# Loading the q and k weights once and copying them by TensorE, and chaining later loads to compute stages, in a fused attention and gMLP block

## The chip, the cores and the metric

The kernel runs on one core of a Trainium2 chip. The core has TensorE (PE, matmuls into the eight banks of PSUM), VectorE (DVE), ScalarE (ACT), GpSimd (POOL) and SyncE (SP). Each runs its own list of instructions in order and waits on semaphores for the others; 16 DMA engines move data between device memory (HBM) and the on-chip memory (SBUF), on transfers that SP and ACT issue here. The metric is the device time of one execution in microseconds (us), and the median of several runs is compared.

## The reference

A block on x of shape (1, 2048, 448), in bf16: sliding, dilated attention with 16 heads of 28 columns, and a gMLP mixer, each behind a layer norm and with a residual.

```python
h = x + A(layernorm(x), wqkv, wo)
h2 = h + B(layernorm(h), w_in, w_sp, b_sp, w_out)

# A: per head, token i attends to i, i-2, ..., i-14 (W=8, dil=2)
idx = pos[:, None] - (jnp.arange(W) * dil)[None, :]
logits = einsum('bhsd,bhswd->bhsw', q, k[..., idx, :]) * 28 ** -0.5
o = einsum('bhsw,bhswd->bhsd', softmax(where(idx >= 0, logits, -1e9)), v[..., idx, :])
return o.reshape(B, S, D) @ wo

# B: F = 1792, Fh = 896
z = gelu(x @ w_in)
z1, z2 = z[..., :Fh], layernorm(z[..., Fh:])
g = einsum('ts,bsf->btf', w_sp, z2) + b_sp[None, :, None]
return (z1 * g) @ w_out
```

## The kernel before

**Tiling.** The 2048 tokens are two halves of 1024. Block u holds 128 tokens of the first half and block u+8 those of the second; the two are worked on together. After the layer norm, TensorE transposes the pair (L643) so that `xh` holds the 448 features as seven chunks of 64, the first half's in partitions 0 to 63 and the second half's in 64 to 127. A matmul over 64 features runs for s = 0 on the lower partitions and for s = 1 on the upper ones. So every weight that multiplies `xh` must stand in both partition halves: q, k (`wqp`, `wkp`), v (`wv`) and `w_in`. A halo of the last 16 tokens of the first half (`xhalo`, `thalo`) goes ahead of the second half's tokens.

**Stages.** (1) Loads, the layer norm of each pair (`bn1`, `rs1` on POOL at L611/L612, `nrm1`), transposes and their eviction. (2) q and k in three token chunks (`mmk`, `mmq`, L738), v for each of nine attention tiles (`mmv`, L778). Per tile: logits (`mml`, L813), exp on ACT (`exp`, L826), a band mask on DVE (`mask`, L833), row sums (`mmr`, L842), ln and exp for the reciprocal, the weighted sum (`mmo`, L862) and its scaling (`ot`, L880). (3) Output projection (`mmy`, L918), residual (`h`), second layer norm and transposes. (4) z2 (`mmz2`, L938, gelu `ge`) and z1 (`mmz1`, L982, `gz1`), the third layer norm; then the big product with `w_sp` (L1019), the gating on DVE (`ua`, `um`) and the output matmuls (`wo`, L1048), stored block by block.

**What sets the order.** A planner in the kernel's own Python lists tasks with durations, dependencies and priorities, and lays them on the five engines; the order so found is the order of the instructions. `OFF`, `TU`, `WPEN`, `MPEN`, `SEED` and `SIGMA` set the priorities. Several evictions may go to either of two or three engines (`alts`). The planner's own estimates are not waits: an instruction waits only for semaphores that its reads and writes need (`Sched.issue`).

**Weights of q and k.** `ld_w("qk", s)` loads the same 448 x 896 columns twice, once into each partition half of `stqk` (which lies in the later `z2p`), one on SP's queue and one on ACT's. Eight copies (`rp`, L702 to L706, on ACT, DVE or POOL) then spread each head's 28 columns to a pitch of 32 in `wqp` and `wkp`.

**Later loads.** `w_in` comes in four transfers of 784 KB (two column halves, two partition halves), `w_sp` in 32 transposing transfers into `wspT_lo` and `wspT_hi`. At the end a list `pace` adds planner dependencies, so that these loads take their place in SP's list behind certain stages:

```python
pace = [by[n % i] for i in range(NT) for n in (("exp%d_0", "ot%d") if i else ("ot%d",))]
later = [t_win[1, 0], t_win[1, 1], t_win[0, 0], t_win[0, 1]] + [t_wsp[b][0] for b in S_ORDER]
for t, d in zip(later, pace):
    t.deps.append(d)
```

No semaphore stands behind these dependencies: on the chip SP issues the transfers as soon as it reaches them.

## Time and profile before

| | |
|---|---|
| median of 3 runs | 274.48 us (272.98 to 274.57) |
| the profiled execution | 273.63 us |
| its span, first to last instruction | 271.7 us |
| mean granted TensorE clock | 0.962 |
| bytes read from HBM / written | 9.20 MB / 1.84 MB |

The span is what the profile shows; the 1.9 us between it and the execution's time lie around it. In the profile's rows a line such as L738 is a line of the kernel above; "out<-in" are names of tiles (`reg` is the shared memory in which `wqp`, `kT`, `E` and others lie; `z2p` holds the staged weights at the start). "[1.60 <-issue]" means that the engine stood idle 1.60 us before the row and that the profile shows nothing it waited for. The granted clock is a share of TensorE's full speed.

These pieces of the chain of waits (start, us, engine and line) date the later stages: z2, the first products with `wspT_lo`, and the long run of them.

```profile
102.76 1.46 PE psum L938 x14
...
120.62 2.75 PE psum L938 x28
123.37 10.59 PE psum L982 x98
...
134.51 0.38 PE psum L1019
...
151.86 10.74 PE psum L1019 x49
...
178.57 1.32 PE psum L1048 x7
```

### The profile page before, as it was taken

How to read it: one execution, taken by the hardware profiler on the slowest of the kernel's cores; microseconds unless marked ns; L12 is line 12 of the kernel's file. 1: busy time of each engine (PE TensorE's matmuls, PEld its weight loads, DVE VectorE, ACT ScalarE, POOL GpSimd, SP SyncE). 2: the span in 40 equal slices, each digit the busy share in tenths (PEclk: the TensorE clock that was granted, in tenths of full speed). 3: DMA queues.
4: the chain of work that ended last, by engine and by line, in shares of the span. 5: the costliest groups of instructions: out<-in, count | busy, mean ns of one | idle time of the engine just before them, and what ended most of it. 6: DMA issues, size and time to landing. Idle time of an engine off the chain costs nothing.

```text
span 271.7 us, 6639 instructions
## 1 busy us (share of the span) xinstructions
PE 253.5 (93%) x2987; PEld 129.5 (48%) x2999; DVE 149.5 (55%) x283; ACT 90.7 (33%) x100; POOL 33.2 (12%) x78
## 2 busy tenths in 40 slices
PE   7279897799999989999999999999999999999995
PEld 2076465344556655544454444444444444444442
DVE  2396993356897877999963133324334423343333
ACT  0068835655489758657657300000000000000000
POOL 7253410000112111232311000000000000000000
PEclk9759997799999979999999999999999999999999
DMA  6960299999900000006444335321000100001002
GB/s 183 250 196 17 54 212 203 165 172 147 188 20 2 2 5 2 0 17 205 72 92 86 80 77 80 77 56 51 2 0 0 51 19 0 0 17 53 0 0 69
DMA packets 43733, 19.85 MB, mean 73 GB/s; under 512 B 34537, under 2 KB 43577, under 8 KB 43705
## 3 DMA queue, kind: packets, MB, share of 16 engines
q1 hardware_dynamic: 42632, 18.11, 33.1%
q10 hardware_dynamic: 1072, 1.32, 1.9%
q8 instruction: 23, 0.38, 0.6%
q14 instruction: 6, 0.04, 0.1%
HBM read 9.20 MB, written 1.84 MB: 41 GB/s over the span
## 4 chain that ended last, share of the span: by engine, by line
PE 85%; DVE 5%; DMA 4%; issue 2%; ACT 2%; POOL 1%; SPq 0%
PE psum L1019 35%; PE psum L738 11%; PE psum L938 8%; PE psum L1048 8%; PE psum L982 8%; PE psum L918 4%; DMA xhalo<-in_A_x_dram 4%; PE psum L813 3%; PE psum L778 3%; PE psum L643 2%; PE psum L862 2%; DVE st L621 1%; ACT reg L826 1%; DVE tring L632 1%; PE psum L842 1%
## 5 line engine op out<-in xcount | busy, mean ns | idle before, releaser
L1029 DVE TENSOR_TENSOR ub<-psum,reg 128x512 bf16<-128x512 f32 x28 | 19.4, 692 | 73.4 <-PE psum L1019 73.4
L1019 PE MATMUL psum<-reg,z2p 128*128 128x512 bf16 x218 | 48.7, 379 | 0.3
L1019 PE MATMUL psum<-wspT_lo,z2p 128*128 128x512 bf16 x218 | 48.4, 379 | 0.4 <-issue 0.2
L1019 PEld LDWEIGHTS psum<-reg,z2p 128*128 128x128 bf16 x224 | 21.9, 98 | 26.2
L1019 PEld LDWEIGHTS psum<-wspT_lo,z2p 128*128 128x128 bf16 x224 | 21.7, 98 | 26.1 <-issue 0.4
L738 PE MATMUL psum<-xh,reg 64*128 64x128 bf16 (+3 forms) x336 | 29.8, 338 | 1.1 <-DVE xh L683 0.9
L1048 PE MATMUL psum<-reg 128*128 128x448 bf16 x112 | 22.3, 352 | 0.0
L938 PE MATMUL psum<-w_in,xh 64*128 64x448 bf16 x224 | 22.3, 349 | 0.0
L606 ACT ACTIVATE reg<-psum 128x896 bf16<-128x896 f32 (+4 forms) x20 | 16.8, 842 | 14.7 <-PE psum L738 8.6
L982 PE MATMUL psum<-xh,w_in 64*128 64x512 bf16 x196 | 21.5, 375 | 0.0
L738 PEld LDWEIGHTS psum<-xh,reg 64*128 64x128 bf16 x336 | 15.8, 110 | 10.6 <-issue 1.1
L621 DVE BATCH_NORM_STATS2 st<-x_tm 128x6 f32<-128x448 bf16 x32 | 19.5, 608 | 2.0 <-DMA x_tm<-in_A_x_dram 1.9
L826 ACT ACTIVATE reg<-psum 128x928 bf16<-128x928 f32 x18 | 17.1, 947 | 8.5 <-PE psum L778 5.9
L954 DVE BATCH_NORM_STATS2 st<-z2p 128x6 f32<-128x448 bf16 x32 | 17.6, 604 | 2.6 <-ACT z2p L948 2.6
L611 POOL TENSOR_SCALAR rs<-mv 128x2 f32<-128x2 f32 x24 | 6.1, 252 | 103.4 <-DVE mv L622 78.2
L948 ACT ACTIVATE z2p<-psum 128x896 bf16<-128x896 f32 x16 | 14.7, 917 | 9.6 <-PE psum L938 9.2
L612 POOL TENSOR_TENSOR rs<-rs,nhalf 128x2 f32<-128x2 f32 x24 | 17.6, 732 | 2.0
L632 DVE TENSOR_SCALAR tring<-x_tm,mv,rs 128x448 bf16<-128x448 bf16 x32 | 15.0, 490 | 3.4 <-POOL rs L612 3.2
L992 ACT ACTIVATE reg<-psum 128x1024 bf16<-128x1024 f32 x14 | 14.3, 1023 | 7.1 <-PE psum L982 7.1
L1048 PEld LDWEIGHTS psum<-reg 128*128 128x128 bf16 x112 | 11.0, 98 | 10.6
L938 PEld LDWEIGHTS psum<-w_in,xh 64*128 64x128 bf16 x224 | 10.9, 94 | 10.1 <-issue 0.8
L778 PE MATMUL psum<-reg,xh 64*64 64x448 bf16 x252 | 14.9, 378 | 0.5 <-DVE xh L608 0.5
(62 smaller groups left out, 229.3 us busy)
## 6 DMA issues: line engine op xcount, KB each, us to landing
w_in<-in_B_w_in_dram SPq DMA_DIRECT2D x4, 784.0 KB, 12.4
out_dram<-tring SPq DMA_DIRECT2D x16, 112.0 KB, 1.7
x_tm<-in_A_x_dram SPq DMA_DIRECT2D x15, 112.0 KB, 8.7
z2p<-in_A_wqkv_dram SPq DMA_DIRECT2D x1, 784.0 KB, 10.2
z2p<-in_A_wqkv_dram ACTq DMA_DIRECT2D x1, 784.0 KB, 11.6
reg<-in_B_w_out_dram SPq DMA_DIRECT2D x1, 784.0 KB, 4.8
reg<-in_B_b_sp_dram SPq DMA_DIRECT2D x1, 512.0 KB, 3.6
reg<-in_A_wqkv_dram ACTq DMA_DIRECT2D x1, 392.0 KB, 7.3
```

The lines of the kernel that those rows point to most:

```text
L612: iss("pool", lambda e: e.tensor_tensor(dst, dst, nh, ALU.pow), reads=rr + [r_nhalf], writes=rr)
L621: iss("dve", lambda e: e.bn_stats(st[:, b, :], x_tm[:, b, :]), reads=[r_x[b]], writes=[rl[b]])
L632: iss("dve", lambda e: e.tensor_scalar(tring[:, h[0], :].rearrange("p (c s f) -> p s c f", c=NC7, s=2)[:, n], x_tm[:, b, :].rearrange("p ( ...
L738: iss("pe", lambda e, c=c, s=s, gi=gi, lhs=lhs: e.matmul(psum[:, bk[s] * 512 + cw * gi:bk[s] * 512 + cw * gi + cw], lhs, xh[64 * s:64 * s ...
L778: iss("pe", lambda e, c=c, s=s, w=w: e.matmul(psum[64 * w:64 * w + 64, bk[s] * 512:bk[s] * 512 + D], xh[64 * s:64 * s + 64, c, a + w:a + w ...
L826: iss("act", lambda e: e.activation(E[:, es[0], 2 * n:2 * n + 2, :], pair_view(lb, 0, 8 * JW), AF.Exp, scale=SCALE), reads=[r_bank[lb[0]], ...
L938: iss("pe", lambda e, c=c, s=s: e.matmul(psum[:, zb[s] * 512:zb[s] * 512 + D], xh[64 * s:64 * s + 64, c, HALO + 128 * u:HALO + 128 * u + 128],
L954: iss("dve", lambda e, b=b: e.bn_stats(st3[:, b, k, :], z2p[:, b, D * k:D * k + D]), reads=[r_z2[b][k]], writes=[r_st3[b][k]])
L982: iss("pe", lambda e, c=c, s=s: e.matmul(psum[:, bk[s] * 512:bk[s] * 512 + 512], w_in[64 * s:64 * s + 64, c, 128 * f:128 * f + 128], xh[64 ...
L1019: iss("pe", lambda e, b=b: e.matmul(psum[:, gb[0] * 512:gb[0] * 512 + 512], z2p[:, b, 128 * f:128 * f + 128], src[:, b, 512 * (tc % 2):512 ...
L1029: iss("dve", lambda e: e.tensor_tensor(ub[:, us_[0], :], psum[:, gb[0] * 512:gb[0] * 512 + 512], bb[:, 512 * tc:512 * tc + 512], ALU.add), ...
L1048: iss("pe", lambda e, f=f: e.matmul(psum[:, wb[0] * 512:wb[0] * 512 + D], z1p[f][:, 128 * m:128 * m + 128], w_out[:, f, :], start=(f == 0) ...
```

## The change

Four things change.

1. The q and k weights are loaded once, 128 features to a partition row: 384 features in one transfer on ACT's queue (`wqk0`), the last 64 on SP's (`wqk1`). The halo moves to second place on SP.
2. A 128 x 128 matrix `dup` with ones on the diagonal and 64 off it is made on POOL. A matmul with half of it as the stationary operand puts 64 features into both partition halves of PSUM: 14 matmuls of 448 columns (`dpk`, `dpq`). Eight evictions (`rp`, now on ACT or DVE) write them to `wkp` and `wqp`. The q/k matmuls now wait for all four pieces of a weight.
3. `w_in` comes in eight transfers (four or three chunks of 64 features). Each load of two chains, `w_in` then the first half of `w_sp`, and bias, `w_out` then the second half of `w_sp`, now waits on semaphores: for the landing of the load before it in its chain and for one stage of compute. The first chain's stages are `exp`, `mask`, `ot` of the tiles in turn, the second's `ge`, `gz1` and `ua`.
4. The planner's priorities have other values, so the order of work changes on all engines.

```diff
-WPEN = 189.727
+WPEN = 200
...
-SEED, SIGMA = 806416, 0.5
+SEED, SIGMA = 242706, 1.0
...
-TU = 7.616
+TU = 7.37
...
+    def mark(self, eng):
+
+        m = Res("mark")
+        m.writes = {eng: self.cnt.get(eng, 0)}
+        return m
...
                     t.emit()
+                    if t.mark is not None and not t.nbytes:
+                        t.mark.append(self.marker(t.eng))
...
-        stqk = z2flat[:, 0:NC7 * 2 * D].rearrange("p (c n) -> p c n", c=NC7)
+        stqk = z2flat[:, 0:4 * 2 * D].rearrange("p (c n) -> p c n", c=4)
...
             def em():
-                key, _ = iss(eng, fn, reads=reads, writes=writes, prod="dma", inc=16)
+                rd = list(reads)
+                for w in t.waits:
+                    if w.nbytes:
+                        rd.append(w.mark)
+                    else:
+                        rd += w.mark
+                key, n = iss(eng, fn, reads=rd, writes=writes, prod="dma", inc=16)
+                t.mark = Res("mark")
+                t.mark.writes = {key: n}
...
+        def ld_win(z, prio):
+            for s in range(2):
+                for c0, c1 in ((0, 4), (4, 7)):
+                    t = dma("sp", "win%d_%d%d" % (z, s, c0), lambda e, s=s, c0=c0, c1=c1: e.dma_start(
+                        w_in[64 * s:64 * s + 64, c0:c1, FH * z:FH * z + FH],
...
-        ld_w("qk", 0, "sp", 0.02)
-        ld_w("qk", 1, "act", -10.0)
-        t_xhalo = dma("sp", "xhalo", lambda e: e.dma_start(xhalo[:, :], X[ST - 16:ST, :]), 16 * D * 2, prio=0.03, writes=[r_xhalo])
+        t_xhalo = dma("sp", "xhalo", lambda e: e.dma_start(xhalo[:, :], X[ST - 16:ST, :]), 16 * D * 2, prio=0.01, writes=[r_xhalo])
+        t_w["qk", 0] = dma("act", "wqk0", lambda e: e.dma_start(
+            stqk[:, 0:3, :], A_wqkv[0:384, 0:2 * D].rearrange("(c p) n -> p c n", p=128)),
+            384 * 2 * D * 2, prio=-11.0, writes=[r_wqk[0]], bw=300.0)
+        t_w["qk", 1] = dma("sp", "wqk1", lambda e: e.dma_start(stqk[0:64, 3, :], A_wqkv[384:448, 0:2 * D]),
+                           64 * 2 * D * 2, prio=0.02, writes=[r_wqk[1]])
...
+        c_dup = cst("c_dup", [(lambda e: e.memset(dup[:], 0.0), [], [r_dup])] + [
+            (lambda e, d=d: e.affine_select(dup[:], dup[:], [[1, 128]], ALU.not_equal, 1.0, base=d, channel_multiplier=-1),
+             [r_dup], [r_dup]) for d in (0, 64, -64)], 1.2, prio=-98.8)
...
-            for g in range(4):
-                tk = []
-
-                def em(p=p, g=g, tk=tk):
-                    c0 = 112 * g + (D if p == "k" else 0)
-                    copy(tk[0].eng, (wqp if p == "q" else wkp)[:, :, 128 * g:128 * g + 128]
+            for j in range(4):
+                bk, tk = [], []
+                hs = range(2 if j < 3 else 1)
+                c0 = D if p == "k" else 0
+
+                def em(j=j, bk=bk, hs=hs, c0=c0):
+                    for h in hs:
+                        iss("pe", lambda e, h=h: e.matmul(psum[:, bk[h] * 512:bk[h] * 512 + D], dup[64 * h:64 * h + 64, :],
+                                                          stqk[64 * h:64 * h + 64, j, c0:c0 + D]),
+                            reads=[r_wqk[j // 3], r_dup], writes=[r_bank[bk[h]]])
+                tm = add("dp%s%d" % (p, j), "pe", 0.2, em, deps=[t_w["qk", j // 3], c_dup], prio=4.0 + n + 0.1 * j,
+                         acq=[("ps", 2, bk)], mode="P", nmm=2)
...
-                             t_wp[p][g0:g0 + ng],
+                             t_wp[p],
...
-        pace = [by[n % i] for i in range(NT) for n in (("exp%d_0", "ot%d") if i else ("ot%d",))]
-        pace += [by["ge%d_%d" % (u, k)] for u in range(3) for k in range(2)]
-        later = [t_win[1, 0], t_win[1, 1], t_win[0, 0], t_win[0, 1]] + [t_wsp[b][0] for b in S_ORDER]
-        for t, d in zip(later, pace):
-            t.deps.append(d)
+
+        def chain(loads, steps):
+            assert len(steps) >= len(loads)
+            for n, t in enumerate(loads):
+                t.deps.append(steps[n])
+                t.deps += loads[n - 1:n] if n else []
+                t.waits += [steps[n]] + (loads[n - 1:n] if n else [])
+                steps[n].mark = steps[n].mark or []
+        pace = [by[n % i] for i in range(NT) for n in ("exp%d_0", "mask%d", "ot%d")]
+        later = t_win[1] + t_win[0] + [t_wsp[b][0] for b in S_ORDER]
+        chain(later, pace)
```

On PE the start of the program reads so before (L643 and L676 are the transposes of the first tokens and of the halo, L738 q/k, L778 v, L813 logits):

```order
L600 MATMUL psum<-warm 128x512 x16
L643 MATMUL psum<-ident,tring 128x128 x7
L676 MATMUL psum<-ident,thalo 128x16 x7
L738 MATMUL psum<-xh,reg 128x128 x112
L778 MATMUL psum<-reg,xh 64x448 x28
L813 MATMUL psum<-reg 64x58 x48
L643 MATMUL psum<-ident,tring 128x128 x7
L813 MATMUL psum<-reg 64x58 x16
```

and so after the change, where L739 is the copying with `dup`, L782 q/k, L822 v and L857 logits:

```order
L632 MATMUL psum<-warm 128x512 x16
L675 MATMUL psum<-ident,tring 128x128 x7
L708 MATMUL psum<-ident,thalo 128x16 x7
L739 MATMUL psum<-z2p,dup 128x448 x12
L822 MATMUL psum<-reg,xh 64x448 x28
L739 MATMUL psum<-z2p,dup 128x448 x2
L782 MATMUL psum<-xh,reg 128x128 x56
L675 MATMUL psum<-ident,tring 128x128 x7
L782 MATMUL psum<-xh,reg 128x128 x56
L822 MATMUL psum<-reg,xh 64x448 x28
L857 MATMUL psum<-reg 64x58 x32
```

The v matmuls of the first tile moved ahead of q/k, inside the copying; the second transposes moved between k and q, and the second v matmuls ahead of the logits.

On SP, from the last `wo` load on, with the semaphores each waits for, before (L887 `wo`, L544 `w_in`, L899 `w_sp`):

```order
L887 DMA reg<-in_A_wo_dram 28x4x448 [waits sem_q23]
L544 DMA w_in<-in_B_w_in_dram 64x7x896 x4
L899 DMA_TRANSPOSE wspT_lo<-in_B_w_sp_dram 128x1024 x16
L1000 DMA reg<-in_B_b_sp_dram 128x2048 [waits sem_pe,sem_q24]
L998 DMA reg<-in_B_w_out_dram 128x7x448 [waits sem_q45]
```

and after, where `sem_q` with a number is the landing of an earlier load and `sem_act`, `sem_dve` count the steps of ACT and DVE:

```order
L931 DMA reg<-in_A_wo_dram 28x4x448 [waits sem_q23]
L568 DMA w_in<-in_B_w_in_dram 64x4x896 [waits sem_act]
L568 DMA w_in<-in_B_w_in_dram 64x3x896 [waits sem_q25,sem_dve]
L568 DMA w_in<-in_B_w_in_dram 64x4x896 [waits sem_q26,sem_dve]
L568 DMA w_in<-in_B_w_in_dram 64x3x896 [waits sem_q27,sem_act]
...
L941 DMA_TRANSPOSE wspT_lo<-in_B_w_sp_dram 128x1024 [waits sem_q32,sem_dve]
L941 DMA_TRANSPOSE wspT_lo<-in_B_w_sp_dram 128x1024 [waits sem_q33]
```

The 20 loads that stood without any wait now each wait for the one before, and most for a stage too. Further down, the last of `wspT_lo` stands behind the bias (which waits for `ge4_0`), and the last two transposes of the second half stand behind the first two stores of the output.

On POOL, the constants `ones` and `mband` moved from ahead of the first `rs1` to behind `rs1` and the halo's `rsh`, and `dup`'s memset and three selects stand ahead of it.

More of the change, by code (lines that the diff above doesn't have):

```diff
@@ L32 @@
 PHASES = [(range(0, 9), range(0, 8))]
[L33 to L38 removed]
+WPEN = 200
+MPEN = 4.643
+OFF = {"q": -58.54, "v": -31.79, "evv": 49.4, "l": -93.27, "exp": 72.79, "mask": 0.56, "r": -59.26,
+       "o": -77.13, "ln": -52.39, "ot": 62.17, "y": -39.74, "h": -34.52, "ln2": -22.88, "z2": 23.16,
+       "ge": -41.5, "n3": -30.02, "x0": -57.55, "xd": 5.33, "evq": 32.44}
+SEED, SIGMA = 242706, 1.0
 O_AFTER_LN = True
 NBANKS = 8
[L41 removed]
+TU = 7.37
 NE = 2
@@ L152 @@
     __slots__ = ("name", "eng", "dur", "emit", "deps", "prio", "acq", "rel", "mode", "epoch",
-                 "gate", "nbytes", "start", "end", "succ", "ndep", "rt", "nmm", "alts")
+                 "gate", "nbytes", "start", "end", "succ", "ndep", "rt", "nmm", "alts", "bw", "waits", "mark")
     def __init__(self, name, eng, dur, emit, deps=(), prio=0.0, acq=(), rel=(), mode=None,
@@ L169, in __init__ @@
         self.nmm = nmm
+        self.bw = 215.0
+        self.waits = []
+        self.mark = None
         self.alts = alts
@@ L190, in add @@
         t = Task(*a, **k)
-        if SIGMA and t.eng != "sp":
+        if SIGMA and not t.nbytes:
             t.prio += self.rng.gauss(0.0, SIGMA)
@@ L219, in pe_time, with run @@
         return max(t.dur, (t.nmm - credit) * self.ISSUE)
-    def run(self, bw=200.0, setup=1.9, t0=0.7):
+    def run(self, setup=1.6, t0=0.7):
         import heapq
@@ L451, in bass_sequential_preLN__sliding_local_dilated__mixer_gmlp__prompt_kernel @@
         r_xend = Res("xend")
-        r_wq = {p: [Res("wqkv_%s%d" % (p, s)) for s in range(2)] for p in ("qk", "v")}
+        r_wv = [Res("wv%d" % s) for s in range(2)]
+        r_wqk = [Res("wqk%d" % s) for s in range(2)]
         r_wo = Res("wo")
-        r_win = [[Res("w_in%d_%d" % (z, s)) for s in range(2)] for z in range(2)]
+        r_win = [[Res("w_in%d_%d" % (z, s)) for s in range(4)] for z in range(2)]
         r_q = [[Res("q%d_%d" % (c, g)) for g in range(4)] for c in range(3)]
@@ L470, in bass_sequential_preLN__sliding_local_dilated__mixer_gmlp__prompt_kernel @@
         r_ident = Res("ident")
+        r_dup = Res("dup")
         r_ones = Res("ones")
@@ L478, in bass_sequential_preLN__sliding_local_dilated__mixer_gmlp__prompt_kernel @@
         r_ln3 = [Res("ln3_%d" % b) for b in range(NB)]
-        r_wp = {p: [Res("w%sp%d" % (p, g)) for g in range(4)] for p in "qk"}
-        reg1_old = r_wq["v"] + r_wp["q"] + r_wp["k"]
-        stg_old = r_wq["qk"]
+        r_wp = {p: [Res("w%sp%d" % (p, j)) for j in range(4)] for p in "qk"}
+        reg1_old = r_wv + r_wp["q"] + r_wp["k"]
+        stg_old = r_wqk
         reg2_old = [r for rr in r_q + r_k for r in rr] + [r_qend, r_kend] + r_OT
@@ L1072, in bass_sequential_preLN__sliding_local_dilated__mixer_gmlp__prompt_kernel @@
         later = [t_bb, t_wout] + [t_wsp[b][1] for b in S_ORDER]
-        for t, d in zip(later, pace):
-            t.deps.append(d)
+        chain(later, pace)
         pl.run()
```

72 lines of the change are left out of this document (35 added, 37 removed).

## Prediction

> **What bounds the kernel now.** I read the page first, then the chain of waits, then the clock and busy time in stretches of 3.41 us, then the timeline of the stretches that stood out.
>
> ```profile
> span 271.7 us, 6639 instructions
> PE 253.5 (93%) x2987; PEld 129.5 (48%) x2999; DVE 149.5 (55%) x283; ACT 90.7 (33%) x100; POOL 33.2 (12%) x78
> ...
> PEclk9759997799999979999999999999999999999999
> ...
> q8 instruction: 23, 0.38, 0.6%
> ...
> z2p<-in_A_wqkv_dram SPq DMA_DIRECT2D x1, 784.0 KB, 10.2
> z2p<-in_A_wqkv_dram ACTq DMA_DIRECT2D x1, 784.0 KB, 11.6
> ...
> reg<-in_A_wqkv_dram ACTq DMA_DIRECT2D x1, 392.0 KB, 7.3
> ```
>
> TensorE (PE) is busy for 93% of the span, so time can only come from its idle 18 us, from stretches at a reduced clock, or from work taken off it. PEclk shows where the clock falls: slices 2 and 3 (6.8 to 20.4 us), 7 and 8 (40.8 to 54.3) and 15 (95 to 102). Behind slice 20 the kernel is one solid run of matmuls; a microsecond won ahead of it stays won, unless a load comes late there.
>
> ```profile
> 1.24 0.73 SPq L536
> ...
> 2.02 9.71 DMA xhalo<-in_A_x_dram
> ...
> 15.41 5.67 PE psum L738 x109
> 21.08 1.45 PE psum L778 x28
> ...
> 40.09 1.28 PE psum L643 x21
> ...
> 43.42 1.60 issue
> ...
> 52.13 1.55 issue
> ...
> 1.23 0.69 ACTq L536 DMA_DIRECT2D reg<-in_A_wqkv_dram  x1
> 1.96 0.64 ACTq L536 DMA_DIRECT2D z2p<-in_A_wqkv_dram  x1
> ```
>
> The chain of waits (start, us, what; the last two rows are the timeline of ACT's queue) says two things. The start waits 9.71 us for a 14 KB halo queued behind the weights; the two halves of the q and k weights land at 1.24 + 10.2 = 11.4 and 1.96 + 11.6 = 13.6 us, so q/k matmuls begin at 15.41 only. And twice PE stands still for "issue", waiting for nothing that the profile shows.
>
> ```profile
> 6.77:10.18 3.41, 1.51 (x12) 1.00 1.08 265
> 10.18:13.60 3.42, 0.00 (x0) 0.50 1.12 235
> ...
> 17.00:20.42 3.42, 3.42 (x70) 0.50 0.25 80
> 40.91:44.32 3.41, 2.51 (x91) 1.00 1.06 199
> 44.32:47.73 3.41, 2.71 (x33) 0.50 1.06 207
> 47.73:51.14 3.41, 3.41 (x70) 0.50 1.18 157
> ...
> 20.42:21.08 0.66, 0.66 (x22) 0.48 (x18) 1.00 0.00 0
> ```
>
> Columns: stretch, its length, PE busy (and instructions), granted clock, DMA share, GB/s; the last row is L738 alone and has PEld too. A stretch that PE filled to 79% or less (1.51, 2.51, 2.71 of 3.41) is followed by a stretch at 0.50; only after a full one does the clock return (51.14 and 20.42). Price: a q/k matmul takes 52 ns at half clock (5.67/109, chain), 30 ns at full (0.66/22).
>
> **The two standstills** lie between these rows (timeline of PE, and one stretch):
>
> ```profile
> 42.69 0.73 PE L813 MATMUL psum<-reg 32*64 32x58 bf16 x27
> 45.02 0.30 PE L813 MATMUL psum<-reg 32*64 32x58 bf16 x5 [1.60 <-issue]
> 45.26 2.83 PE L778 MATMUL psum<-reg,xh 64*64 64x448 bf16 x28
> ...
> 49.38 2.54 PE L738 MATMUL psum<-xh,reg 64*128 64x512 bf16 x14
> ...
> 55.72 1.69 PE L738 MATMUL psum<-xh,reg 64*128 64x512 bf16 x14
> ...
> 70.17 1.52 PE L778 MATMUL psum<-reg,xh 64*64 64x448 bf16 x28
> ...
> 45.00:53.60 8.60, 7.11 (x128) 3.12 (x128) 2.65 (x3) 4.28 (x5) 0.00 (x0) 0.64 1.18 168
> 80.00:90.00 10.00, 9.70 (x290) 5.91 (x279) 8.54 (x17) 7.99 (x10) 1.70 (x2) 1.00 0.02 3
> ```
>
> Each stop falls inside a run of like matmuls (27 then 5), and from the first to the second PE ran exactly 128 matmuls and 128 weight loads: 256 instructions. Queue q8 moved 0.38 MB in 23 packets, about 16.5 KB each, 64 bytes per instruction if one packet holds 256. So PE runs dry at the end of a block of its own program, whose next block came late. Both stops fall where the DMA engines are full (shares 1.06 to 1.18): the w_in loads, four of 784 KB issued at once, and the w_sp transposes behind them. At 80 to 90 us, with DMA at 0.02, 569 instructions pass without such a stop.
>
> **The change, part by part.**
>
> 1. *Weights loaded once* (minus 784 KB), issued from ACT right behind the first tokens; the halo is second on SP. The nearest rows for the landing are the first 504 KB of ACT's queue at 8.5 us (1.23 + 7.3) and the first 896 KB of SP's at 11.4; the new piece ends at 784 KB on ACT's queue. Bounds 8.5 to 11.4; I take 9.5, since the SP queue beside it now carries smaller rows.
>
> 2. *Copies on TensorE.* 14 matmuls of 448 columns. L778 does 28 of 448 columns in 1.45 us, so 0.7 to 1.4 us here, at PE's idle start; not the price. The price is their eviction, since only four bank pairs turn: six of 896 columns and two of 448, seven of them on ACT or DVE ahead of the first q/k matmul, where before eight copies ran SBUF to SBUF on three engines.
>
> ```profile
> L606 ACT ACTIVATE reg<-psum 128x896 bf16<-128x896 f32 x9 | 8.3, 919 | 6.0 <-PE psum L778 3.3 <-PE psum L842 1.1 <-PE psum L813 0.8
> L608 DVE CAST reg<-psum 128x768 bf16<-128x768 f32 x3 | 2.9, 954 | 0.4 <-PE psum L738 0.4
> 4.83 0.12 POOL L583 MEMSET ones<- 128x32 bf16 x1
> ...
> 7.06 0.22 POOL L611 TENSOR_SCALAR rs<-mv 128x2 f32<-128x2 f32 x1 [0.17 <-POOL mband L591]
> ...
> 25.23 2.98 PE L778 MATMUL psum<-reg,xh 64*64 64x448 bf16 x56 [0.53 <-DVE xh L608]
> ...
> 29.28 0.39 PE L842 MATMUL psum<-reg,ones 64*32 64x232 bf16 x16 [0.56 <-DVE reg L833]
> ```
>
> POOL's ten instructions for `ones` and `mband` lie between 4.83 and rs at 7.06 (0.22 us each); they move behind rs, and a memset and three selects about half as long again (4 x 0.35 = 1.4 us) come ahead of it: rs comes about 0.8 us sooner, and tokens, halo and PE's first transposes are through at about 9.2 us. So the weights at 9.5 decide. Walk: first copies 9.5; ACT evicts from 10.1, 0.9 us each, three until 12.8, when a pair is free for the V matmuls, which the new order puts ahead of q/k. Clock: 6.77 to 10.18 will again not be full, 10.18 to 13.6 has gaps, so I take half clock until 17.0: V 2.8 us (the slow row of L778 below), to 15.6; last copies 16.0; 56 k matmuls (19 at half clock until 17.0, 37 at full) to 18.1; seven transposes 0.5; 56 q matmuls x 30 ns = 1.7: 20.3. Before, the same work was done at 21.08 + 1.45 = 22.53: **2.2 us**. From there to 40.09 PE needed 17.56 us and stood idle in it 1.1 us (0.53 for L778, 0.56 for L842, the first mask); the new order puts the mask's wait behind five more q/k groups and the L778 wait behind logits: **1.1 us**. DVE, busy from 16.4 us before, starts on block 1 at about 11, so it is not late. Sum of the start: 3.3. Ends: weights at 11.4 leave 1.4; full clock throughout (V 1.3 less, copies and k 0.7 less) gives 5.3.
>
> 3. *Loads one at a time.* w_in now goes in eight pieces (448 and 336 KB) and w_sp in 16 transposes, each behind the landing of the last and a stage of attention. At most 448 KB stand ahead of a program block, 2.2 us at the 200 GB/s of the rows above, where before 3.1 MB did. Gone: 1.60 + 1.55 = **3.15 us**. With it the stretch 40.91 to 44.32 is full, and the half clock of 44.32 to 51.14 goes: L778 2.83 us against 1.52 at full clock, L738 2.54 against 1.69, some small ones 0.3: **2.45 us**. Ends: nothing of either, all of both. The wait costs SP only: behind it stand further loads, and the output stores from about 180 us on. Need dates (chain rows shown ahead of the prediction): w_in from L938's first matmul at 102.76, its first half lands by the new steps before 50; wspT_lo from L1019's first at 134.51, and its last load follows `ge4_0`, in the L938 work that ends at 123.37; wspT_hi from some 30 us behind the last wspT_lo start. Price nothing; cover about 10 us.
>
> 4. *New priorities.* Four evictions move from ACT to DVE between 68 and 101 us (two V, two xh). Up to 2.0 us could go (0.52 + 0.36 idle, and some 1.1 of L918's 2.85 if that is half clock, below), and up to 3.4 come (two V at 0.954 x 896/768 = 1.11 and two xh at 0.6 on DVE, which is 85% busy there by the row of 80 to 90). Neither has a row that decides: 0.
>
> ```profile
> 97.67 0.57 PE L862 MATMUL psum<-reg 64*32 64x58 bf16 x32 [0.52 <-ACT reg L826]
> 98.60 2.85 PE L918 MATMUL psum<-reg 128*128 128x448 bf16 x8 [0.36 <-ACT reg L850]
> ```
>
> Sum: 3.3 + 3.15 + 2.45 = 8.9 us. The profiled execution took 273.63 us (span 271.7): 273.63 - 8.9 = **264.7 us**. Its 273.63 stands 0.85 under the median of the runs, 274.48.
>
> **Rivals.**
>
> *A. The program blocks still come late.* A piece of 448 KB fills all 16 engines just as well; if a block needs the queue empty, the stops only move. Then parts 3's 5.6 us stay: 273.63 - 3.3 = 270.3. For it: pieces start when a mask or an exp ends, near the dense logits. Against: 2.2 us of transfer is less than the some 4.5 us that 256 instructions last at their densest (569 in 10 us). The Trainium skill (Runtime: NRT & Kernel Launch, "Instruction fetch mechanics") holds that fetching is hidden, because the sequencer issues more slowly than blocks are filled; by that rule the stops have another cause and stay, which is this rival. The trace disagrees, with 1.60 and 1.55 us exactly 256 instructions apart.
>
> *B. The stops go, the half clock stays*, since logits and transposes alone leave the array thin: 273.63 - 3.3 - 3.15 = 267.2. The rows can't tell, as the one stretch contains the stop too. The Trainium skill (TensorE: Matmul & The Clock Gate, "Part 4: PE-mode transpose") says transposes don't count as busy like other matmuls; about 1 us of that stretch is transposes, so by it this is the outcome. Rows against: 80 to 90 us has transposes and logits and stays at 1.00.
>
> *C. The start gains nothing*: the eviction chain on ACT and V ahead of q/k eat the earlier weights: 273.63 - 5.6 = 268.0. It needs the weights at about 13 us, or evictions of 1.3 us each instead of 0.92.
>
> *D, the other sign. The w_sp loads now run under the densest stretch*, 68 to 101 us, where DMA stood at 0.02 and a block lasts 4.5 us. If blocks come too late there, each of some six stops PE by 1.6 us, and the clock falls once as before (2.45): 264.7 + 6 x 1.6 + 2.45 = 276.8. Decides: whether a block takes over 4.5 us to come; behind the w_in queue it took 8.7 (45.02 to 52.13 + 1.55). Against: 60 to 70 us had the same transposes back to back (DMA 1.09) and no stop, at 488 instructions per 10 us, so there a block came within 5.2 us, and the new transposes have gaps between them.
>
> ```profile
> 60.00:70.00 10.00, 10.00 (x248) 4.68 (x240) 7.74 (x7) 4.67 (x6) 0.00 (x0) 1.00 1.09 177
> ```
>
> **How the numbers follow.** Forecast 0.43 (its own range, by the ends of the start and part of 4: 261 to 268), A 0.18, B 0.21, C 0.10, D 0.08. The range 260.4 to 271.0 takes in A, B and C and leaves out D and both extremes of 4. About 1% (2.7 us) can be told from no change; against 274.48 faster means under 271.7: the forecast, B, C and most of A, 0.86; same 0.08; slower 0.06.
>
> **What would show it.** Right: first q/k matmuls before 18 us; no "issue" piece of over 1 us in the chain of waits; PEclk at 9 in slices 7 and 8; start of the solid run of L1061 near 143 us instead of 151.9. Wrong: copies starting after 11.4 us; stops 256 instructions apart; PE waiting for wspT_lo or w_in; idle PE between 70 and 100.

## The result, and the profile after

| | before | after |
|---|---|---|
| median of 4 runs each | 274.52 us (272.98 to 275.78) | 266.54 us (265.50 to 267.73) |
| profiled execution, its span | 273.63 us, 271.7 us | 266.21 us, 264.5 us |
| granted clock over the span | 0.962 | 0.994 |

The ratio of the times is 0.9713, 95% interval 0.9648 to 0.9779. Run again beside later experiments the changed kernel took 265.94 us (263.98 to 271.92, 6 runs), ratio 0.9662 (0.9605 to 0.9719). The forecast was 264.7, in a range of 260.4 to 271.0. A run over 1.5% above its kernel's fastest counts in the medians but not in the ratios; of E2 below only one run is under that bound, so it has no ratio, and the profiled executions of E2 and E11 are over it.

These lines of the page of the changed kernel answer to those shown of before: span, engines, granted clock by slices, the queue of instructions, the load of the weights.

```profile
span 264.5 us, 6703 instructions
...
PE 252.7 (96%) x3001; PEld 129.2 (49%) x3013; DVE 151.3 (57%) x284; ACT 91.2 (34%) x101; POOL 34.5 (13%) x80
...
PEclk9999999999999799999999999999999999999999
...
q8 instruction: 23, 0.38, 0.6%
...
z2p<-in_A_wqkv_dram ACTq DMA_DIRECT2D x1, 672.0 KB, 4.9
```

PE is busy for 252.7 us against 253.5 (the copies come, half clock goes), in a span 7.2 us shorter: its idle time went from 18.2 to 11.8 us. Slices 7 and 8 are at 9; so are slices 2 and 3, which the forecast still had at half clock. Only slice 14 is not. The first 672 KB of weights land 4.9 us after their issue at 1.25 us; before, two loads of 784 KB took 10.2 and 11.6.

The chain of waits of the changed kernel (start, us, what):

```profile
12.80 1.52 PE psum L822 x28
14.61 1.56 PE psum L782 x56
...
34.30 1.28 PE psum L675 x21
...
36.61 0.70 PE psum L857 x28
37.31 1.03 issue
38.57 1.45 PE psum L822 x28
...
116.17 10.59 PE psum L1024 x98
...
144.67 10.74 PE psum L1061 x49
```

L822 is the old L778 (v), L782 the old L738 (q and k), L675 the transposes (L643), L857 the logits (L813), L1024 the old L982 (z1), L1061 the old L1019. The same places in both: the group of 21 transposes starts at 34.30 instead of 40.09 (5.8 us won), z1 at 116.17 instead of 123.37 (7.2), the long run of L1061 at 144.67 instead of 151.86 (7.2). One stop in the instruction stream is left, 1.03 us, in a run of logits again (28 and 4).

Since the two orders interleave the same work differently, I also compared equal amounts of work. Each kind of matmul (line and columns) gets the time that one of it takes in full-clock groups of these traces, the new copies nothing; "lag" is the time at which so much matmul work was done, less that work. Worked out from all matmul records of each trace; the levels depend on these prices, and the differences between rows are good to a few tenths:

```
lag in us at matmul work of      10    20    30    60    80   120 us
before                         17.9  18.9  25.5  27.4  33.5  34.0
after                          12.9  13.1  15.7  18.6  26.4  26.8
after, run again (E9)          12.8  13.1  14.9  17.8  25.7  25.7
E1 after, loads don't wait     15.4  15.7  23.7  26.6  35.0  35.4
E2 before, loads wait          16.9  18.0  19.3  21.1  28.0  35.3
E4 after, old numbers          16.1  16.5  17.2  21.5  30.9  32.0
E5 after, weights twice        17.2  17.4  18.9  21.8  29.6  29.6
E7 after, smaller pieces       14.3  14.6  16.0  18.9  26.9  26.9
E12 after, four on ACT         12.9  13.1  14.8  17.7  27.5  28.8
```

Work 20 is reached at 38.9 us before and 33.1 after, work 30 at 55.5 and 45.7, work 80 at 113.5 and 106.4. Step by step the change won 5.8 us up to work 20 and 4.0 from there to 30 (6.6 of new lag before, 2.6 after), and lost 1.0 from 30 to 60 and 1.7 from 60 to 80: 7.1 in sum.

### The profile page after: what moved, and what is told of

Same layout as the page of the kernel before. It is cut to its first block, busy times and chain, and to the rows that moved or that the text cites. A ratio compares the mean times of both kernels' runs of the same rounds, so it can differ in the third digit from the quotient of the medians.

```text
span 264.5 us, 6703 instructions
## 1 busy us (share of the span) xinstructions
PE 252.7 (96%) x3001; PEld 129.2 (49%) x3013; DVE 151.3 (57%) x284; ACT 91.2 (34%) x101; POOL 34.5 (13%) x80
## 3 DMA queue, kind: packets, MB, share of 16 engines
HBM read 8.39 MB, written 1.84 MB: 39 GB/s over the span
## 4 chain that ended last, share of the span: by engine, by line
PE 89%; DVE 4%; ACT 2%; POOL 2%; issue 2%; POOLq 0%
PE psum L1061 36%; PE psum L782 10%; PE psum L980 8%; PE psum L1090 8%; PE psum L1024 8%; PE psum L960 5%; PE psum L822 4%; PE psum L906 3%; PE psum L675 3%; PE psum L857 2%; DVE reg L924 2%; PE psum L886 1%; ACT reg L870 1%; ACT reg L638 1%; DVE x_tm L968 0%
## 5 line engine op out<-in xcount | busy, mean ns | idle before, releaser
L1061 PE MATMUL psum<-wspT_lo,z2p 128*128 128x512 bf16 x218 | 48.5, 379 | 0.4 <-issue 0.2
L1061 PE MATMUL psum<-reg,z2p 128*128 128x512 bf16 x218 | 48.5, 379 | 0.3
L1061 PEld LDWEIGHTS psum<-reg,z2p 128*128 128x128 bf16 x224 | 21.9, 98 | 26.3
L1061 PEld LDWEIGHTS psum<-wspT_lo,z2p 128*128 128x128 bf16 x224 | 21.7, 98 | 26.1 <-issue 0.4
L782 PE MATMUL psum<-xh,reg 64*128 64x128 bf16 (+3 forms) x336 | 26.8, 306 | 0.5 <-ACT reg L870 0.5
L638 ACT ACTIVATE reg<-psum 128x896 bf16<-128x896 f32 (+5 forms) x25 | 20.3, 849 | 13.4 <-PE psum L739 6.4
L1090 PE MATMUL psum<-reg 128*128 128x448 bf16 x112 | 22.2, 352 | 0.0
L870 ACT ACTIVATE reg<-psum 128x928 bf16<-128x928 f32 x18 | 17.0, 943 | 14.0 <-PE psum L857 6.3
L1024 PE MATMUL psum<-xh,w_in 64*128 64x512 bf16 x196 | 21.5, 375 | 0.0
L643 POOL TENSOR_SCALAR rs<-mv 128x2 f32<-128x2 f32 x24 | 7.9, 331 | 99.0 <-DVE mv L654 69.4
L782 PEld LDWEIGHTS psum<-xh,reg 64*128 64x128 bf16 x336 | 13.4, 93 | 10.0 <-ACT reg L870 0.6
L960 PE MATMUL psum<-reg 128*128 128x448 bf16 x64 | 14.6, 374 | 2.4 <-DVE reg L924 1.7
L640 DVE CAST reg<-psum 128x1024 bf16<-128x1024 f32 (+4 forms) x12 | 12.9, 1073 | 6.3 <-PE psum L782 5.4
```

The lines of the kernel that those rows point to most:

```text
L638: iss("act", lambda e: e.activation(dst, src, AF.Copy), reads=rd, writes=wr)
L782: iss("pe", lambda e, c=c, s=s, gi=gi, lhs=lhs: e.matmul(psum[:, bk[s] * 512 + cw * gi:bk[s] * 512 + cw * gi + cw], lhs, xh[64 * s:64 * s ...
L870: iss("act", lambda e: e.activation(E[:, es[0], 2 * n:2 * n + 2, :], pair_view(lb, 0, 8 * JW), AF.Exp, scale=SCALE), reads=[r_bank[lb[0]], ...
L960: iss("pe", lambda e, s=s, g=g: e.matmul(psum[:, bk[s] * 512:bk[s] * 512 + D], qT[:, s, g, 128 * u:128 * u + 128], wo_p[:, g, :], start=(g ...
L1024: iss("pe", lambda e, c=c, s=s: e.matmul(psum[:, bk[s] * 512:bk[s] * 512 + 512], w_in[64 * s:64 * s + 64, c, 128 * f:128 * f + 128], xh[64 ...
L1061: iss("pe", lambda e, b=b: e.matmul(psum[:, gb[0] * 512:gb[0] * 512 + 512], z2p[:, b, 128 * f:128 * f + 128], src[:, b, 512 * (tc % 2):512 ...
```

## The experiments

**E1 and E2: the waits alone.** E1 takes the semaphores away from the changed kernel and leaves every order; E2 gives them to the kernel before.

```diff
 # E1, in dma() of the changed kernel
-                for w in t.waits:
+                for w in ():
 # E2, in dma() of the kernel before
+                for w in t.waits:
+                    rd += w.mark
+                if t.line:
+                    rd.append(t.line[-1])
```

> The changed kernel with the same order on every engine, but the chained loads no longer wait on semaphores, neither for a stage nor for the landing of the load ahead. Theory (program blocks of 256 instructions come late behind queued loads): two stops of 1.0 to 1.7 us return between 33 and 55 us, 256 PE instructions apart, with a stretch at half clock behind them: 266.2 plus 3 to 5.6, so 269 to 272. Rival (the new order of work took the stops away, not the waits): no stop of over 1.1 us, 266 to 267.

> The kernel before with the same order on every engine; the chained loads only wait, each for its stage and for the landing of the load ahead; the four w_in pieces stay 784 KB. Theory: the stops of 1.60 and 1.55 us and the half clock behind them (2.45) go, or one shorter stop of about 1 us stays because a piece of 784 KB still holds the engines for some 5 us: 273.6 less 3 to 5.6, so 268 to 271. Rival (waits alone do nothing, the stops stay where they were): 273 to 275.

E1 took 272.25 us (271.01 to 274.81, 10 runs), ratio to before 0.9882 (0.9849 to 0.9914); by the ratios 5 to 6 us are lost by the waits' absence. One stop came instead of the two expected. Timeline of PE in E1:

```profile
39.13 0.77 PE L857 MATMUL psum<-reg 32*64 32x58 bf16 x28
44.28 0.26 PE L857 MATMUL psum<-reg 32*64 32x58 bf16 x4 [4.38 <-issue]
44.47 2.83 PE L822 MATMUL psum<-reg,xh 64*64 64x448 bf16 x28
```

The stop is at the same place as in the changed kernel, behind 28 of 32 logits, but it lasts 4.38 us instead of 1.03. The 2.83 us of L822 (1.45 in the chain above) are the half clock behind it, which the trace shows from 42.0 to 48.9 us. From work 20 to 30 E1 gained 8.0 of lag, the changed kernel 2.6 (1.8 when run again).

In E2 both stops are gone, and the clock stays full from 18.95 to 90.6 us: 1.3 of lag from work 20 to 30, where before had 6.6. That is 5.3 won in the old order of work. Yet E2 took 275.05 us (270.80 to 276.14, 4 runs), above the 268 to 271 that its theory expected. Its timeline of ACT and then of PE, from the profiled execution:

```profile
132.66 3.26 ACT L1014 ACTIVATE reg<-psum 128x1024 bf16<-128x1024 f32 x3 [7.67 <-DMA reg<-in_B_w_out_dram]
```

```profile
128.98 0.38 PE L1041 MATMUL psum<-wspT_lo,z2p 128*128 128x512 bf16 x1
133.83 0.90 PE L665 MATMUL psum<-ident,tring 128*128 128x128 bf16 x7 [4.47 <-ACT reg L1014]
```

ACT's fifth gelu of z1 writes over the same old memory as `w_out` and so waits for that load, which now stands behind the chained `w_sp` loads on SP's queue and behind the bias load: issued at 127.97 it lands at 132.6. PE stands 4.5 us for it, and a stretch at half clock (131.6 to 138.4) follows: 7.3 of lag between work 80 and 120, more than the 5.5 that E2 was ahead of before at work 80.

**E3: is it the place in the program?** 64 more PE instructions at the very start, in a bank that is idle there.

```diff
+            for _ in range(32):
+                iss("pe", lambda e: e.matmul(psum[:, w_hold[0] * 512:w_hold[0] * 512 + 16], warm[:, 0:128], warm[:, 0:16]),
+                    reads=[r_warm], writes=[r_bank[w_hold[0]]])
```

> The kernel before with 32 more matmuls of 16 columns behind the 16 that warm the array, so 64 more PE instructions at the very start, where PE waits for data anyway. Theory (a stop lies at a boundary of 256 instructions): the first stop moves 64 instructions earlier in the program, out of the L813 run of 27 and 5 into the run of seven transposes ahead of it, the second by as much, still 256 apart. Rival (the stop belongs to those instructions, by a wait that the profile does not show): it stays after 27 of the 32 L813 matmuls. Time by both within 1% of before.

275.17 us (273.64 to 277.25, 8 runs), ratio 1.0023 (0.9977 to 1.0069). The logits of 27 and 5 run through; one stop is left, and it is here (timeline of PE):

```profile
45.17 1.03 PE L741 MATMUL psum<-xh,reg 64*128 64x512 bf16 x7
49.64 1.89 PE L741 MATMUL psum<-xh,reg 64*128 64x512 bf16 x7 [3.43 <-issue]
```

Counted over all of PE's records (matmuls, weight loads and 5 or 6 records of its sequencer) it falls at instruction 1473, where the second stop of before fell, and that is 64 instructions earlier in the program. In before, in the changed kernel and in E1 the first falls at 1217 = 1473 - 256. So the count decides, not the instruction. The first stop did not move but vanished: 64 instructions earlier its block was fetched at 32.96 to 34.04 us, while SP was still issuing the `w_in` loads (31.72 to 35.83). That part of the expectation was wrong, in a way that the same mechanism explains.

Packets of the instruction queue against PE's stops (us; "asked" is when PE passes the instruction 256 ahead of the block; that this is the request is my reading; ahead of the `w_in` loads and from 60 us on, the fetches of before and after begin mostly within 2 us of it, a few up to 1.6 us ahead of it, so that the request itself must lie somewhat earlier):

```
                 asked   fetch    PE stops, goes on
before           37.81   42.14-43.53   43.42, 45.02
                 45.02   51.41-52.41   52.13, 53.68
E1               35.54   41.43-42.83   39.90, 44.28
E3               40.76   46.69-48.10   46.20, 49.63
after            32.95   35.69-36.88   37.31, 38.34
after again E9   32.94   34.78-36.05   none
E7               34.43   36.34-37.36   none
E8               34.57   35.03-36.44   none
E2               36.82   37.61-38.99   none
```

A fetch takes 1.0 to 1.4 us, and PE goes on 1.3 to 1.5 us behind its end. What differs is the wait ahead of it: 4.3 to 6.4 us in the rows with loads issued in a bundle, 0.5 to 2.7 in those where each load waits for the last. In E8 no load was in flight at 34.57 us (one piece had landed at 31.34, the next was issued at 38.08), and its wait is the shortest. At the block after these the chained kernels waited up to 3.4 us (E13) without a stop.

**E4 and E10: the numbers that set the order.** E4 puts the old ones into the changed kernel, E10 the new ones into the kernel before.

```diff
-WPEN = 200
-MPEN = 4.643
+WPEN = 189.727
+MPEN = 4.564
...
-SEED, SIGMA = 242706, 1.0
+SEED, SIGMA = 806416, 0.5
```

> The changed kernel with the numbers that set the order taken back to those of before (penalties, offsets, seed and noise, pace per tile); loads, waits and copies stay as changed. Theory (the new order costs the 2.7 us that the stretch from 60 us to the first L982 matmul lost): that stretch takes 53.6 us instead of 56.3 and the time is 263 to 265, if the start does as well. Rival (the old numbers do not suit the new start and loads): as late or later, 266 to 270, with the idle time of 0.5 us ahead of the second V group and the first mask back.

> The kernel before with the numbers that set the order taken from the changed kernel (penalties, offsets, seed and noise, pace per tile); loads, weights and copies as before. Theory (these numbers suit the new start and cost some 2 us between 60 and 105 us): not faster, 273 to 277, with the stops for program blocks still there. Rival (the new order is a gain by itself, as the changed kernel with the old numbers being 5 us slower could suggest): 269 to 272.

E4: 271.31 us (270.77 to 271.59, 4 runs), ratio 0.9854 (0.9815 to 0.9894), about 5 slower than the changed kernel and above what either side had expected. Its lag is 3.4 larger by work 20 and 4.5 by work 80; it also meets the late `w_out` (landed 138.66, ACT idle for 4.80 us). E10: 283.02 us (282.29 to 285.76, 4 runs), ratio 1.0365 (1.0284 to 1.0445). Its chain and its timeline of PE at the start:

```profile
1.24 10.30 DMA z2p<-in_A_wqkv_dram
...
11.56 1.27 DVE reg L608 x2
```

```profile
15.71 0.93 PE L643 MATMUL psum<-ident,tring 128*128 128x128 bf16 x7 [9.10 <-DVE tring L632]
```

DVE copies the late weights ahead of the first normalization, and PE waits 9.10 us; the time is above both expectations. Either set is worth much with the loads that it was made for and costs 5 (E4) or 8 to 10 us (E10, by medians and by the ratio) with the others; neither has a value of its own.

**E5 and E13: the start.** E5 brings the weights twice again in the changed kernel, with eight copies from SBUF to SBUF in place of TensorE's; E13 adds one load that nothing reads, ahead of the second unit's tokens.

```diff
 # E5
-            stqk[:, 0:3, :], A_wqkv[0:384, 0:2 * D].rearrange("(c p) n -> p c n", p=128)),
+                stqk[64 * s:64 * s + 64, :, :], A_wqkv[:, 0:2 * D].rearrange("(c p) n -> p c n", p=64)),
 # E13
+        dma("sp", "more", lambda e: e.dma_start(
+            z2flat[:, 4 * 2 * D:7 * 2 * D].rearrange("p (c n) -> p c n", c=3), A_wqkv[0:384, 0:2 * D].rearrange("(c p) n -> p c n", p=128)),
```

> The changed kernel, but the q and k weights come twice again, 784 KB on SP behind the halo and 784 KB on ACT, and eight copies from SBUF to SBUF on three engines replace the TensorE copies; the order numbers, the chained loads and the early halo stay. Theory (the single load is what starts the q and k matmuls earlier): weights land at 11 to 13.6, first q/k matmuls at 15 to 16 with PE idle ahead of them, the start some 2 to 3 us later than the changed kernel's: 268 to 270. Rival (the start is set by evictions and V, or what is lost there is caught up by 60 us): within 1 us of the changed kernel, 265.5 to 267.5.

> The changed kernel with one load more: 672 KB of the q and k weights a second time, into a part of z2p that nothing reads, on SP ahead of the second unit's tokens; the order on PE, ACT, DVE and POOL is the same. Theory (from the first tile to the transposes at 34 us PE goes at the pace of DVE's normalization, so the start is won by the tokens that land 2.9 us sooner): tokens of units 1 to 7 land 2 to 3 us later, and PE is 1.5 to 3 us later from the second group of transposes on, with waits for DVE: 268 to 269.5. Rival (the start is won by q and k weights alone): first q/k matmuls and the rest within 0.7 us of the changed kernel, 265.5 to 267.

E5: 272.24 us (269.75 to 272.81, 4 runs), ratio 0.9895 (0.9833 to 0.9958), above both expectations. Timeline of PE:

```profile
20.98 0.56 PE L670 MATMUL psum<-ident,tring 128*128 128x128 bf16 x7 [0.27 <-DVE tring L659]
22.96 1.52 PE L807 MATMUL psum<-reg,xh 64*64 64x448 bf16 x28 [1.42 <-DVE xh L635]
...
26.07 0.56 PE L670 MATMUL psum<-ident,tring 128*128 128x128 bf16 x7 [0.99 <-DVE tring L659]
```

The q and k matmuls begin earlier than expected, at 11.9 us, but at half clock (10.6 to 17.4), and what is late afterwards is DVE's normalization of the next units (2.7 us of waits in these rows): 4.3 of lag at work 20. The half clock has a part in that; the changed kernel's profiled execution had none there. The second unit's normalization starts here, behind copies of the weights (timeline of DVE in before, then in the changed kernel; E5: 14.26):

```profile
13.99 1.25 DVE L608 COPY reg<-z2p 128x784 bf16<-128x784 bf16 x2
...
15.28 1.16 DVE L608 COPY reg<-z2p 128x784 bf16<-128x784 bf16 x2
16.36 0.60 DVE L621 BATCH_NORM_STATS2 st<-x_tm 128x6 f32<-128x448 bf16 x1
```

```profile
9.93 1.09 DVE L640 CAST reg<-psum 128x896 bf16<-128x896 f32 x1
10.94 0.62 DVE L653 BATCH_NORM_STATS2 st<-x_tm 128x6 f32<-128x448 bf16 x1
```

It starts 5.4 us sooner. The unit's tokens don't hold it up: they had landed at 12.62 and 13.12 us before, and at 9.15 and 9.58 after. What stands ahead of it in DVE's list does: before, the halo (landed at 11.73) and four copies of weights that were there only at 13.54; after, the evictions of the weights that TensorE copied. E13 was to test whether late tokens set the pace: 269.06 us (267.77 to 270.05, 4 runs), ratio 0.9833 (0.9762 to 0.9904), inside what the theory expected, but not by its mechanism. Issues of loads in E13, with the time to landing:

```profile
x_tm<-in_A_x_dram SPq DMA_DIRECT2D x15, 112.0 KB, 6.9
...
z2p<-in_A_wqkv_dram SPq DMA_DIRECT2D x1, 672.0 KB, 7.6
```

The last tokens landed at 16.21, and at 14.26 to 15.75 in the six other executions with this start: 0.5 to 1.9 us later, not 2 to 3. Those of the second unit were there at 10.22 and 10.85, and DVE began on them at 10.93, as without the load. PE's first wait for a normalized unit is 0.28 us long, as in the changed kernel; the later start in the profile (1.6 at work 10) goes with a half clock from 13.0 to 16.4 us. So E13 doesn't decide what later tokens would cost. That DVE's own list sets the pace when the weights come late rests on E5's waits and the DVE rows.

**E7, E8, E9: the stop that was left.** E7 halves the first four `w_in` pieces; E8 holds the second piece until the first tile's output stands (`ot0`), and each later one a stage longer; E9 is the changed kernel unaltered.

```diff
 # E7
-                for c0, c1 in ((0, 4), (4, 7)):
+                for i, (c0, c1) in enumerate(((0, 2), (2, 4), (4, 6), (6, 7)) if z else ((0, 4), (4, 7))):
 # E8
-        chain(later, pace)
+        chain(later, pace[:1] + pace[2:])
```

> The changed kernel with its first four w_in pieces (448 and 336 KB) cut into eight (224 and 112 KB), each behind the landing of the last, a stage waited for at every second one only; same order on PE, ACT, DVE and POOL. Theory (a program block waits for the one load that is in flight when it is asked for): the fetch that began 2.74 us after its request begins within 1.5 us, the stop of 1.03 us at PE instruction 1217 goes: about 265.3 against 266.3 profiled. Rival (piece size is not what holds the block): the stop stays and the time is the same. Other sign: the chain of loads runs some 4 us longer, w_out lands after the fifth gelu of z1 wants its place, and the time is 0.5 to 3 us longer.

> The changed kernel, but from the second w_in piece on each load waits for one stage later in the list, so the second piece is issued near 36 us instead of 32.0, behind the request of the program block at 32.95; same order on PE, ACT, DVE and POOL. Theory: that block is fetched at once and the 1.03 us stop goes, with none in its place if the next block, asked for at about 36, comes by 43: about 265.3 profiled. Rival (blocks come late for another reason): stop stays, 266.3. Other sign: loads end some 4 us later, and w_out misses the fifth gelu of z1 by up to 4 us: 267 to 270.

> The changed kernel unaltered, for comparison in the same call. Both theories: 265.5 to 267.7, one stop of about 1 us at PE instruction 1217. If the half clock at the start, which an earlier experiment showed, comes and goes from run to run, some runs lie 2 to 3 us above the others.

E7: 267.34 us (266.64 to 269.72, 6 runs), ratio 0.9746 (0.9694 to 0.9798). E8: 269.89 (267.78 to 272.80, 6 runs), ratio 0.9836 (0.9768 to 0.9904). Neither profile has the stop; but nor has E9's, where the fetch started 1.84 us after its request instead of 2.74. So the 1.03 us are not there in every execution, and E7 and E8 can't show that they removed it; in E7 the fetch began 1.9 us after it was asked for, not within the 1.5 expected. Both lost some 1.5 at the start, where their profiled executions were granted half clock for 3.4 us, ahead of anything that they change; and in E8 `w_out` came late again (ACT idle for 3.94 us, PE for 0.73). Neither beats the changed kernel.

**E11 and E12.** E11 is E2 with the waits on the first chain alone; E12 hands the four evictions that the new order gave to DVE back to ACT, in place.

```diff
 # E11, at the second chain only, against E2
-            t.waits.append(d)
-            t.line = line
 # E12
-                copy(tev[0].eng, xh[:, :, HALO + 128 * u:HALO + 128 * u + 128],
+                copy("act" if which == 2 and u in (2, 3) else tev[0].eng, xh[:, :, HALO + 128 * u:HALO + 128 * u + 128],
...
-                copy(tk[0].eng, V[:, vs[0], :, :, 0:DH], pair_view(bk, 0, D).rearrange("p s (h d) -> p s h d", d=DH),
+                copy("act" if i in (5, 7) else tk[0].eng, V[:, vs[0], :, :, 0:DH], pair_view(bk, 0, D).rearrange("p s (h d) -> p s h d", d=DH),
```

> The kernel before with the same order on every engine; only the first chain of loads (w_in and the first half of w_sp) waits for stages and landings; the bias, w_out and the second half of w_sp are issued as before. Theory: the two stops and the half clock behind them go as in the earlier run with both chains (5.9 us by the time of the third tile), and the 4.36 us in which PE and ACT waited for w_out near 130 us go too: 267 to 269 profiled. Rival (what the waits win at 45 us is lost later whatever the second chain does): 271 to 275.

> The changed kernel with four evictions (V of tiles 5 and 7, normalized tokens of units 2 and 3) run by ACT instead of DVE at the same places; order on PE the same. Theory (they make DVE late and cost the stretch 60 to 105 us some 2 us): PE's waits for L924 of DVE (0.48 and 0.62 us) shrink, 264 to 265 profiled. Rival (the chain from the sums over exp to L924 is late by itself): within 0.7 us of the changed kernel, 265.5 to 267.

E11: 273.25 us (270.02 to 277.48, 12 runs), ratio 0.9924 (0.9874 to 0.9974); stops gone, the wait near 130 us still there (4.23 us of idle PE), so that by the ratio only some 2 us are won. So the late `w_out` does not come from the second chain's own waits: SP takes its list in order, and `w_out` stands behind the chained loads. The expectation that it would go was wrong. E12: 267.35 us (266.14 to 269.24, 6 runs), ratio 0.9772 (0.9708 to 0.9837): no gain, and slightly above the rival's 265.5 to 267. Its timeline of PE:

```profile
81.97 3.12 PE L960 MATMUL psum<-reg 128*128 128x448 bf16 x8 [0.83 <-DVE reg L924]
...
101.92 1.69 PE L960 MATMUL psum<-reg 128*128 128x448 bf16 x8 [0.62 <-DVE reg L924]
```

and that of the changed kernel at the same places:

```profile
82.88 1.69 PE L960 MATMUL psum<-reg 128*128 128x448 bf16 x8 [0.82 <-DVE reg L924]
...
100.75 1.50 PE L960 MATMUL psum<-reg 128*128 128x448 bf16 x7 [0.62 <-DVE reg L924]
```

The two longest waits for L924 are the same with four evictions less on DVE (the 3.12 us of L960 are half clock). The evictions are not what PE waits for there.

## Why the prediction came out

**Parts 1 and 2, the start: right in sign and in its steps, under-sized (5.8 instead of 3.3, above its upper end of 5.3).** The walk holds but for its clock. The weights landed at 7.27, not 9.5, but PE had transposes until then, and the first copies started at 9.50 as forecast. The end of q and k was forecast for 20.3, with half clock until 17.0. It came at 19.8 to 20.0 where 3.4 us of half clock were granted (E7, E8, E13), at 20.9 with 6.8 us of it (E1), and at 18.3 or 18.4 where the clock stayed full (the changed kernel, E9, E12). The last q matmuls in the changed kernel and then in E13 (timeline of PE):

```profile
16.61 1.75 PE L782 MATMUL psum<-xh,reg 64*128 64x128 bf16 x56
```

```profile
18.25 1.75 PE L785 MATMUL psum<-xh,reg 64*128 64x128 bf16 x56
```

So the mis-sized term is the half clock: 2.0 of the 2.5 us missed, and it is a matter of the execution. With the half clock of E7 the start wins 4.3. The other 0.5 is about the second unit's transposes, which the walk to 20.3 has behind it and the kernel before at 22.53 had not. "Starts on block 1 at about 11, so it is not late" held for DVE (10.94). What the forecast did not price is how late DVE becomes when the weights are late: E5 puts parts 1 and 2 at 4.3 us of lag by work 20, with 2.7 us of PE's waits for DVE in it, and with its own half clock.

**Part 3, the stops: the mechanism was right, and its size nearly.** Predicted 5.6, got 4.0 from work 20 to 30 in the first profile, and 4.8 when run again without the 1.03 us stop. E1 gives back 5.4 against the first and 6.2 against the second; E2 wins 5.3 in the old order. Without the stop, what is short of 5.6 is near the 0.5 us that PE newly waits there for an exp (L782 behind L870). "At most 448 KB stand ahead of a block, 2.2 us" was about the wait measured (2.74 and 1.84), but the 1.3 to 1.5 us between a block's landing and PE's first instruction from it were in no term. The rule read off three stretches (PE busy for 79% or less, then half clock) does not hold throughout the trace of before: from 51.14 to 54.55 us PE was busy for 1.86 of 3.41 us, with the second stop in it, and full clock followed. That the half clock from 44.32 on went with the stops is shown by E1 and E2. Rival A (blocks late as ever) falls by E1 and E2. Rival B (half clock stays) falls as well: with the stops gone E2 keeps full clock from 18.95 to 90.6, and with the stop back E1 has half clock from 42.0. Rival C falls by the start, D by the fetches at 68 to 101 us, which started within 1.4 us of their requests with `w_sp` loads under way.

**"Price nothing; cover about 10 us" was the step that happened to hold.** I took the need dates of `w_in` and `w_sp` and left out `w_out`, which is behind them on SP. In the changed kernel it was issued at 119.00, landed at about 123.7, and the gelu that waits for it started at 123.80: cover 0.1 us (1.1 in E9). In E2, E4, E8 and E11 it is missed, at up to 4.5 us of idle PE and, in E2 and E11, a half clock behind it. It is missed in E12 and E13 as well (landed at 128.07 and 127.65), which leave that chain as it is. So the step held by luck, and not in every execution.

**Part 4, the order: "0" was wrong in kind.** It has no price of its own. With the new loads the old numbers cost 5 us (E4), with the old loads the new ones cost 8 to 10 (E10). Inside the changed kernel the stretch from work 30 to 80 lost 2.7 us against before. I had named four evictions on DVE as what could cost up to 3.4; E12 speaks against them: PE's idle time from work 30 to 80 is 2.6 us in both, and the 2.0 of lag that E12 has more there goes with 10.2 us of half clock instead of 3.4. What the stretch lost stays open in the main. PE's idle time rose by 0.7 only (from 1.9 before), for which the chain from the row sums over ln and exp to L924 is enough; both kernels were granted 3.4 us of half clock in it. Where the other 2 us lie is not shown.

The median came out 1.8 us over the forecast; in the profiled executions 2.5 more at the start were set against 1.6 less by the stops and 2.7 lost later: 8.9 + 2.5 - 1.6 - 2.7 = 7.1. That the forecast came so near is in part luck, since these three errors offset each other. Of the signs named, the first q/k matmuls (14.45 us, before 18) and slices 7 and 8 came; "no issue piece of over 1 us" failed by 0.03 in the first profile and held in E9's.

## What to carry to other kernels

If an engine stops for nothing inside a run of like instructions, count the instructions between stops; if they are a multiple of one block, look at what loads were issued in a bundle ahead, and let each wait for the last. When loads are slowed so, check the need date of everything behind them in the same queue, also of loads that are waited for only because memory is reused. An order tuned for one arrival of data is part of that design: price it together with the loads, and in the start follow the engine that prepares the data (here DVE and what stands ahead in its list), not only the one that computes.

## What the runs showed of the hardware that was not expected

- A block of 256 PE instructions (16 KB) was fetched in 1.0 to 1.4 us, but behind bundled loads the fetch began 4.3 to 6.4 us after PE had passed the instruction 256 ahead, and PE went on only 1.3 to 1.5 us after it ended. Stops of 1.55 to 4.38 us came of it; with a wait of 2.7 us one of 1.03 was left, and with 1.9 or less none.
- The form of a load mattered as well as its bytes: with a second load of 672 KB over 128 partitions (E13) the last tokens landed at 16.21 us, and with the weights loaded twice over 64 partitions each (E5), 784 KB more in all, at 18.44; without either they landed at 14.26 to 15.75.
- The clock is granted in steps of 3.41 us whose phase to the program differs in each execution. Four of seven executions with the changed start were granted half clock in it and three were not, with the same PE instructions. In the two thin steps ahead (between 4.5 and 14.2 us, by phase), PE's busy shares by matmul records added up to 1.37, 1.32 and 1.29 in those that kept full clock (after, E12, E9), and to 1.21, 1.20, 1.21 and 1.20 in those that lost it (E7, E1, E8, E13). In later stretches the same sum did not separate them.
